# Block-sparse attention and SwiGLU on one core: scores issued a position earlier, gathers of V behind an exponential, and edge blocks sharing score matmuls

## The chip, the cores and the metric

The kernel runs on one core of a Trainium2 chip. The metric is the device time of one execution in microseconds (us).

## The reference

Two stages follow one another. First comes block-sparse attention over q, k and v of shape (4 batches, 8 heads, 768 positions, 64): the sequence is cut into 24 blocks of 32, and a query block sees its own block and the two beside it, the first and the last block, and three sampled blocks; the first and the last query block see everything.

```python
mask = np.abs(blk_i - blk_j) <= window
mask = mask | (blk_i == 0) | (blk_j == 0) | (blk_i == n_blocks - 1) | (blk_j == n_blocks - 1)
for qb in range(n_blocks):
    for kb in sampled_blocks[qb]:
        mask[qb * block:(qb + 1) * block, kb * block:(kb + 1) * block] = True
scores = np.where(mask, scores, -1000000000.0)
...
attn = attn / (np.sum(attn, axis=-1, keepdims=True) + 1e-09)
```

Its output, with the heads laid side by side, is x: 3072 tokens of 512. Then comes a feed-forward stage: RMS normalisation with a gain, two products with 512 x 1536 weights, SwiGLU, and a product with 1536 x 512 weights.

```python
rms = np.sqrt(np.mean(x * x, axis=-1, keepdims=True) + 1e-06)
xn = x / rms * rms_g
g = xn @ w_gate
silu = g * (1.0 / (1.0 + np.exp(-g)))
val = xn @ w_val
return (silu * val @ w_out).astype(np.float32)
```

## The kernel before

Everything is in bfloat16 with sums in float32. Batch 0 is computed densely with a mask, in three query groups, and fills the first 73 us or so; the change does not touch it. Batches 1 to 3 are cut into 18 chunks of four query blocks (128 rows). Fifteen chunks are narrow: four neighbouring blocks, whose 128 keys per block (window, first and last block, sampled blocks; each key row holds two neighbouring positions) are gathered into a tile of their own. Three are edge chunks, one in each batch: blocks 0, 23, 1 and 22, of which the first two see the whole sequence.

The order of the work is written out by hand. A loop runs over 19 steps (i = 0 to 18), each with ten positions (0 to 9). At each position it issues the jobs that were put down for it with `do(position, job)`, and then `position()` issues as many pieces of the feed-forward stage (FFN) as a rate says, so that TensorE has matrix work between the small pieces of attention. The FFN runs on groups of 2, 3, 4, 4, 3 and 2 chunks (256, 384 or 512 columns); its pieces are gate (gp, L737, then a tanh on ScalarE, th, L741), value (vp, L748, then two products on VectorE, u, L752, and hps, L756) and down (yp, L766, four pieces to a chunk, then ScalarE's yo, L771, and a store by SyncE's queue). Engines run their instructions in the order of issue.

What step i issues for chunk i, for the chunk before and for the one after (nx = i + 1):

- position 0: `values(i - 1)`, two halves of four heads (op, L644), on TensorE; positions 1 and 2: `normalise` of each half (rz, L669, and stage, L670) on VectorE; 4: `squares` (L677) on ScalarE; 5: `rms_power` (add L681, power L682) on GpSimd; 7: `x_scaled` (xs, L698 or L695) on VectorE, which reads the power, followed by a transposing DMA or, for some chunks, by transposes on TensorE.
- positions 1 to 4, in edge chunks 1 to 8: `scores(i, part)`. A part is one burst: eight score matmuls of 64 columns (L620) into one PSUM bank, and then at once the exponential of that bank on ScalarE (ex, L628), 512 columns. A narrow chunk has four parts of two heads, an edge chunk eight parts of one head. In an edge chunk's part, six of the eight matmuls go over the whole sequence (three thirds of the keys, straight from KT, for block 0 and for block 23) and two over gathered keys (kg) of blocks 1 and 22.
- for the next chunk: queries to a block-diagonal tile (`gather_q`, L500 or L503, VectorE, positions 3 and 5), window and edge keys (`gather_k`, L471 and L476, VectorE, positions 4 and 6), sampled keys (`sampled_k`, L485, GpSimd at position 0 and ScalarE spread over the step) and the rows of V (`gather_v`, L512): up to four indirect DMAs, issued by GpSimd at position 2. A tile of gathered V rows is used by every second chunk, so the gathers for chunk i + 1 wait for the values of chunk i - 1.
- for the next batch: loads on GpSimd's queue (L126, position 9), casts and transposes of keys and queries (L455 on TensorE, L457 on ScalarE), a table of V in DRAM.

Score, value, gate, down and transpose results share eight PSUM banks. `bank()` hands them out in a ring: three banks, one, and four more, in fixed order; whoever writes the bank next waits until its last reader is done. Three tiles hold exponentials (four parts each).

Of the kernel before, what the change touches and what calls it, by code (L numbers as in the profile page):

```python
# [18 lines left out]
def kernel(  # L19
# [495 lines left out]


# [89 lines left out]

    def bursts(i):
        return 8 if chunks[i][1][0] == 0 else 4

    def scores(i, part):  # L610
        b, qbs = chunks[i]
        wide = qbs[0] == 0
        heads = H // bursts(i)
        st = bank([P, 512], FP32, "st")
        at = 0
        for h in range(part * heads, (part + 1) * heads):
            of = [(KT[b % 2][:, h, cc::HC], j) for cc in range(HC) for j in range(2)] if wide else []
            of += [(kgs[i % 2][:, h, j, :], j) for j in range(2 if wide else 0, QB)]
            for lhsT, j in of:
                nc.tensor.matmul(  # L620
                    out=st[:, at:at + UN], lhsT=lhsT,
                    rhs=Qd[i % 2][:, h, :, :, j * HB:(j + 1) * HB].rearrange("p a w s -> p (a w) s"),
                    start=True, stop=True)
                at += UN
        if part % 4 == 0:
            exs[(i, part // 4)] = work.tile([P, 4 * 512], BF16, name="ex", tag="ex", bufs=3)
        ex = exs[(i, part // 4)][:, part % 4 * 512:(part % 4 + 1) * 512]
        nc.scalar.activation(  # L628
            out=ex.rearrange("p (u s w) -> p u s w", s=HB, w=2),
            in_=st.rearrange("p (u w s) -> p u s w", s=HB, w=2), func=AF.Exp, scale=SCALE)  # L630
# [3 lines left out]
    def values(i, g):  # L634
        b, qbs = chunks[i]
        wide = qbs[0] == 0
# [10 lines left out]
        for h in range(4 * g, 4 * g + 4):  # L647
            part = h // per
            ex = exs[(i, part // 4)][:, part % 4 * 512:(part % 4 + 1) * 512].rearrange(
                "p (h u w s) -> p h u w s", h=per, w=2, s=BLK)[:, h % per]  # L650
            if not wide:
# [3 lines left out]
                continue  # L655
            for n in range(NC):
                cc, w = divmod(n, 2)
                for j in range(2):
                    mm(h, j, ex[:, 2 * cc + j, w, :], Vs[b % 2][:, 2 * cc + w, h, :], n, NC)
                if n < 2:  # L660
                    for j in range(2, QB):
                        mm(h, j, ex[:, 4 + j, n, :], vg[:, j, n, h, :], n, 2)
# [415 lines left out]
    for i in range(NCH + 1):  # L1078
# [30 lines left out]
        if i < NCH:  # L1109
            n = bursts(i)  # L1110
            for part in range(n):
                do(1 + part, lambda part=part: scores(i, part))
# [10 lines left out]
        if nx is not None:  # L1123
# [20 lines left out]
            if nx > 1:  # L1144
                do(2, lambda: gather_v(nx))
# [51 lines left out]
```

## Time and profile before

| | us |
|---|---|
| median of three runs | 290.3 |
| lowest, highest | 289.85, 290.57 |
| the profiled execution, its own time | 290.28 |
| its span in the profile | 288.5 |

The span is the time from the first to the last instruction; 1.8 us of the profiled execution lie around it. The granted TensorE clock was 1.0 throughout. In the rows, PE is TensorE's matmuls, PEld its weight loads, DVE VectorE, ACT ScalarE, POOL GpSimd. A row of a timeline has the start, the duration, the engine, the line, the operation, its tiles (written <- read), the shape and a count; a bracket at its end has the idle time of the engine before it and what ended it. Tiles may show the name of a larger tile in which they lie: wide_q and wide_k hold the queries, keys and gathered keys of every second chunk. In a row of groups stand the total busy time and the mean of one in ns.

### The profile page before, as it was taken

The numbers are of one execution on the slowest core, as the hardware profiler recorded it, in microseconds if no ns is written. First come the engines' busy times: TensorE is split into PE (matmuls) and PEld (weight loads), VectorE is DVE, ScalarE is ACT, GpSimd is POOL, SyncE is SP. The second block draws the span as 40 slices with busy tenths as digits, with TensorE's granted clock in tenths as the row PEclk, the third lists the DMA queues.
The fourth block names the chain that finished last, engine by engine and source line by source line (L and its number), as shares of the span: only waits on it lengthen the run. The fifth ranks groups of instructions, "written<-read, shape, count | busy, mean of one in ns | idle before, by whom it ended". The sixth has DMA issues, their size and how long they took to land.

```text
span 288.5 us, 9875 instructions
## 1 busy us (share of the span) xinstructions
PE 273.9 (95%) x3840; PEld 185.3 (64%) x3871; DVE 216.7 (75%) x596; ACT 198.2 (69%) x467; POOL 146.7 (51%) x244
## 2 busy tenths in 40 slices
PE   8798999898999899799999999999999999999995
PEld 6586896687668678666665555545545556664783
DVE  7888889678979959966999578796499951784580
ACT  4896786588589789759989878577746484533331
POOL 8857244558487585787887627627723330101000
PEclk9999999999999999999999999999999999999999
DMA  7999999999885479898995845426932252000102
GB/s 133 287 214 201 206 207 268 290 229 315 168 232 125 142 205 287 173 222 259 250 170 154 280 122 154 101 73 186 204 115 77 59 168 77 36 2 36 75 1 73
DMA packets 37426, 47.44 MB, mean 164 GB/s; under 512 B 11184, under 2 KB 29380, under 8 KB 37380
## 3 DMA queue, kind: packets, MB, share of 16 engines
q0 software_dynamic: 21184, 32.60, 51.1%
q1 hardware_dynamic: 16132, 14.18, 17.2%
q8 instruction: 30, 0.49, 0.7%
q14 instruction: 16, 0.13, 0.1%
q10 hardware_dynamic: 64, 0.03, 0.0%
HBM read 46.45 MB, written 8.83 MB: 192 GB/s over the span
## 4 chain that ended last, share of the span: by engine, by line
PE 64%; DVE 16%; DMA 11%; issue 3%; POOL 3%; ACT 2%; DVEq 0%; ACTq 0%; POOLq 0%
PE yp L766 19%; PE gp L737 16%; PE vp L748 15%; PE st L620 5%; DMA gain<-in_moe_rms_g_dram 5%; DVE u L752 4%; DVE hps L756 4%; DMA qbf<-in_q_dram 4%; PE op L644 4%; DMA vraw<-in_v_dram 3%; PE tqk L455 2%; PE st L527 2%; DVE stage L670 1%; DVE xs L698 1%; PE op L536 1%
## 5 line engine op out<-in xcount | busy, mean ns | idle before, releaser
L512 POOL DMA_INDIRECT vg<-vtab,vidx x66 | 65.5, 992 | 45.2 <-PE op L644 27.1
L737 PE MATMUL gp<-xg,wg 128*128 128x256 bf16 (+2 forms) x426 | 80.2, 307 | 2.2 <-DVE stage L670 0.9
L748 PE MATMUL vp<-xg,wv 128*128 128x256 bf16 (+2 forms) x428 | 80.0, 307 | 1.4 <-DVE u L752 0.6
L741 ACT ACTIVATE th<-gp 128x256 bf16<-128x256 f32 (+2 forms) x108 | 49.8, 463 | 37.6 <-PE gp L737 34.4
L752 DVE SCALAR_TENSOR_TENSOR u<-th,gp 128x256 bf16<-128x256 bf16 (+2 forms) x108 | 54.5, 504 | 22.1 <-ACT th L741 21.5
L766 PE MATMUL yp<-wo,hps 128*128 128x512 bf16 (+1 forms) x282 | 69.1, 370 | 1.6 <-issue 0.3
L756 DVE TENSOR_TENSOR hps<-u,vp 128x256 bf16<-128x256 bf16 (+2 forms) x108 | 55.1, 510 | 11.6 <-PE vp L748 0.5
L628 ACT ACTIVATE ex<-st 128x512 bf16<-128x512 f32 x84 | 50.4, 600 | 13.8 <-PE st L620 12.6
L737 PEld LDWEIGHTS <-wg 128*128 128x128 bf16 x432 | 39.7, 98 | 20.0 <-issue 2.0
L748 PEld LDWEIGHTS <-wv 128*128 128x128 bf16 x432 | 39.5, 98 | 18.6 <-issue 1.5
L766 PEld LDWEIGHTS <-hps 128*128 128x128 bf16 x300 | 26.1, 98 | 20.8 <-DMA wo<-in_moe_w_out_dram 0.3
L530 ACT ACTIVATE ex<-st 128x768 bf16<-128x768 f32 x42 | 33.3, 813 | 5.8 <-PE st L527 5.6
L771 ACT ACTIVATE yo<-yp 128x512 f32<-128x512 f32 (+1 forms) x25 | 14.6, 582 | 19.7 <-PE yp L766 19.5
L681 POOL TENSOR_TENSOR ssq<-ssq,eps 128x1 f32<-128x1 f32 x18 | 4.3, 241 | 39.6 <-ACT junk L677 38.1
L527 PE MATMUL st<-wide_q,wide_k 88*128 88x256 bf16 x144 | 22.9, 272 | 1.5 <-DVE wide_q L345 1.1
L644 PEld LDWEIGHTS <-ex 128*32 128x32 bf16 x1344 | 13.6, 95 | 7.8 <-issue 7.8
L670 DVE TENSOR_TENSOR stage<-op,rz 128x256 bf16<-128x256 f32 x36 | 15.3, 425 | 1.2
L644 PE MATMUL op<-vg,ex 128*32 128x66 bf16 x1056 | 15.2, 195 | 1.0 <-DVE u L752 1.0
L527 PEld LDWEIGHTS <-wide_k 88*128 88x128 bf16 x144 | 13.0, 97 | 5.0 <-DVE wide_q L345 2.0
L620 PEld LDWEIGHTS <-kg 128*128 128x128 bf16 x272 | 12.7, 98 | 5.2 <-issue 0.3
L620 PEld LDWEIGHTS <-wide_q 128*128 128x128 bf16 x256 | 12.5, 98 | 5.3 <-issue 0.2
L620 PE MATMUL st<-wide_q 128*128 128x64 bf16 x256 | 15.1, 193 | 0.1
(147 smaller groups left out, 379.6 us busy)
## 6 DMA issues: line engine op xcount, KB each, us to landing
out_dram<-yo SPq DMA_DIRECT2D x20, 256.0 KB
vraw<-in_v_dram SPq DMA_DIRECT2D x12, 384.0 KB
kbf<-in_k_dram POOLq DMA_DIRECT2D x15, 192.0 KB, 5.7
vtab<-Vs POOLq DMA_DIRECT2D x3, 792.0 KB, 6.2
qbf<-in_q_dram POOLq DMA_DIRECT2D x12, 192.0 KB, 8.4
vraw<-in_v_dram POOLq DMA_DIRECT2D x4, 384.0 KB, 6.4
wg<-in_moe_w_gate_dram POOLq DMA_DIRECT2D x4, 384.0 KB, 10.6
wv<-in_moe_w_val_dram POOLq DMA_DIRECT2D x4, 384.0 KB
```

Of the source, the lines that this page charges most:

```text
L512: nc.gpsimd.indirect_dma_start(vgs[i % 2][:, j, :], None, vtab[b][:], bass.IndirectOffsetOnAxis(ap=vidx[:, qbs[j]:qbs[j] + 1], axis=0))
L527: nc.tensor.matmul(out=at[:, e], lhsT=KT0[0:KR, h, jt * P:(jt + 1) * P], rhs=QT0[0:KR, h, c0 * P:(c0 + 2) * P], start=True, stop=True)
L530: nc.scalar.activation(out=ex[:, 3 * part:3 * (part + 1), :], in_=at[:, 0:3], func=AF.Exp, scale=SCALE)
L620: nc.tensor.matmul(out=st[:, at:at + UN], lhsT=lhsT, rhs=Qd[i % 2][:, h, :, :, j * HB:(j + 1) * HB].rearrange("p a w s -> p (a w) s"), sta ...
L628: nc.scalar.activation(out=ex.rearrange("p (u s w) -> p u s w", s=HB, w=2), in_=st.rearrange("p (u w s) -> p u s w", s=HB, w=2), func=AF.E ...
L644: nc.tensor.matmul(out=op[j * BLK:(j + 1) * BLK, at:at + VW], lhsT=lhsT, rhs=rhs, start=(n == 0), stop=(n == of - 1))
L737: nc.tensor.matmul(out=gp[:, 0:tg], lhsT=wg[:, c, f * P:(f + 1) * P], rhs=xg[:, c, 0:tg], start=(c == 0), stop=(c == KD - 1))
L741: nc.scalar.activation(out=th[:, 0:tg], in_=gp[:, 0:tg], func=AF.Tanh, scale=0.5)
L748: nc.tensor.matmul(out=vp[:, 0:tg], lhsT=wv[:, c, f * P:(f + 1) * P], rhs=xg[:, c, 0:tg], start=(c == 0), stop=(c == KD - 1))
L752: nc.vector.scalar_tensor_tensor(out=u[:, 0:tg], in0=th[:, 0:tg], scalar=1.0, in1=gp[:, 0:tg], op0=ALU.add, op1=ALU.mult)
L756: nc.vector.tensor_tensor(out=hps[f][:, 0:tg], in0=u[:, 0:tg], in1=vp[:, 0:tg], op=ALU.mult)
L766: nc.tensor.matmul(out=yp, lhsT=hps[f][:, tt * P:(tt + 1) * P], rhs=wo[:, f, lo:hi], start=(f == 0), stop=(f == NF - 1))
```

## The change

Four things are done.

1. `scores` and the exponentials become two jobs. In narrow chunks the scores of parts 0 to 3 are issued at positions 0 to 3 (they stood at 1 to 4); in edge chunks at positions 0, 1, 1, 2, 3, 3, 4 and 5 (they stood at 1 to 8). The exponentials stay at 1 + part. In step 0 both stand one position later than that: scores at 1 to 4, exponentials at 2 to 5.
2. In an edge chunk a part's scores over the whole sequence are three matmuls of 128 columns, for blocks 0 and 23 together, in place of six of 64. The two over gathered keys keep 64 columns, which are now written as two runs of 32 side by side with those of the other block. The exponential reads and writes longer runs, and `values` reads the new layout.
3. From step 1 on, the gathers of V for the next chunk are preceded on GpSimd by a copy of one element of an exponential tile (`behind`): part 1 of this step, in edge chunks part 2. It is issued at position 3, in edge chunks 4, and so are the gathers for the next chunk's blocks 0 to 2; they stood at position 2.
4. The gather for the fourth block is issued at position 6, behind the add and the power of `rms_power` at position 5.

VectorE's order is the same in both programs; so is ScalarE's apart from step 0, and SyncE's. GpSimd has 16 instructions more, and 72 matmuls go with their weight loads.

```diff
--- before.py
+++ after.py
@@ -513,6 +513,11 @@
                     vgs[i % 2][:, j, :], None, vtab[b][:],
                     bass.IndirectOffsetOnAxis(ap=vidx[:, qbs[j]:qbs[j] + 1], axis=0))
 
+    gate = const.tile([1, 1], BF16, name="gate")
+
+    def behind(i, part):
+        nc.gpsimd.tensor_copy(out=gate, in_=exs[(i, part // 4)][0:1, part % 4 * 512:part % 4 * 512 + 1])
+
 
     def ex_tile():
         t = work.tile([P, 4 * 512], BF16, name="ex", tag="ex", bufs=3)
@@ -604,36 +609,53 @@
 
     exs = {}
 
+    banks = {}
+
+    def wide(i):
+        return chunks[i][1][0] == 0
+
     def bursts(i):
-        return 8 if chunks[i][1][0] == 0 else 4
+        return 8 if wide(i) else 4
 
     def scores(i, part):
+
         b, qbs = chunks[i]
-        wide = qbs[0] == 0
         heads = H // bursts(i)
-        st = bank([P, 512], FP32, "st")
-        at = 0
+        st = banks[(i, part)] = bank([P, 512], FP32, "st")
         for h in range(part * heads, (part + 1) * heads):
-            of = [(KT[b % 2][:, h, cc::HC], j) for cc in range(HC) for j in range(2)] if wide else []
-            of += [(kgs[i % 2][:, h, j, :], j) for j in range(2 if wide else 0, QB)]
-            for lhsT, j in of:
+            q = Qd[i % 2][:, h].rearrange("p a w s -> p (a w) s")
+            if wide(i):
+                for cc in range(HC):
+                    nc.tensor.matmul(
+                        out=st[:, 2 * cc * UN:2 * (cc + 1) * UN], lhsT=KT[b % 2][:, h, cc::HC],
+                        rhs=q[:, :, 0:2 * HB], start=True, stop=True)
+                for j in range(2, QB):
+                    nc.tensor.matmul(
+                        out=st[:, 2 * HC * UN:].rearrange("p (x j s) -> p x j s", j=2, s=HB)[
+                            :, :, j - 2, :],
+                        lhsT=kgs[i % 2][:, h, j, :], rhs=q[:, :, j * HB:(j + 1) * HB],
+                        start=True, stop=True)
+                continue
+            for j in range(QB):
+                at = ((h % heads) * QB + j) * UN
                 nc.tensor.matmul(
-                    out=st[:, at:at + UN], lhsT=lhsT,
-                    rhs=Qd[i % 2][:, h, :, :, j * HB:(j + 1) * HB].rearrange("p a w s -> p (a w) s"),
-                    start=True, stop=True)
-                at += UN
+                    out=st[:, at:at + UN], lhsT=kgs[i % 2][:, h, j, :],
+                    rhs=q[:, :, j * HB:(j + 1) * HB], start=True, stop=True)
+
+    def exponentials(i, part):
+        st = banks.pop((i, part))
         if part % 4 == 0:
             exs[(i, part // 4)] = work.tile([P, 4 * 512], BF16, name="ex", tag="ex", bufs=3)
         ex = exs[(i, part // 4)][:, part % 4 * 512:(part % 4 + 1) * 512]
+        n = 2 * HB if wide(i) else HB
         nc.scalar.activation(
-            out=ex.rearrange("p (u s w) -> p u s w", s=HB, w=2),
-            in_=st.rearrange("p (u w s) -> p u s w", s=HB, w=2), func=AF.Exp, scale=SCALE)
+            out=ex.rearrange("p (u s w) -> p u s w", s=n, w=2),
+            in_=st.rearrange("p (u w s) -> p u s w", s=n, w=2), func=AF.Exp, scale=SCALE)
 
     ops, stages, ssqs, rstds = {}, {}, {}, {}
 
     def values(i, g):
         b, qbs = chunks[i]
-        wide = qbs[0] == 0
         op = bank([P, 512], FP32, "op")
         ops.setdefault(i, []).append(op)
         vg = vgs[i % 2].rearrange("p j (w h x) -> p j w h x", w=2, h=H)
@@ -646,20 +668,21 @@
 
         for h in range(4 * g, 4 * g + 4):
             part = h // per
-            ex = exs[(i, part // 4)][:, part % 4 * 512:(part % 4 + 1) * 512].rearrange(
-                "p (h u w s) -> p h u w s", h=per, w=2, s=BLK)[:, h % per]
-            if not wide:
+            ex = exs[(i, part // 4)][:, part % 4 * 512:(part % 4 + 1) * 512]
+            if not wide(i):
+                ex = ex.rearrange("p (h j w s) -> p h j w s", h=per, j=QB, w=2)[:, h % per]
                 for w in range(2):
                     for j in range(QB):
                         mm(h, j, ex[:, j, w, :], vg[:, j, w, h, :], w, 2)
                 continue
+            ex = ex.rearrange("p (u w j s) -> p u w j s", w=2, j=2, s=BLK)
             for n in range(NC):
                 cc, w = divmod(n, 2)
                 for j in range(2):
-                    mm(h, j, ex[:, 2 * cc + j, w, :], Vs[b % 2][:, 2 * cc + w, h, :], n, NC)
+                    mm(h, j, ex[:, cc, w, j, :], Vs[b % 2][:, 2 * cc + w, h, :], n, NC)
                 if n < 2:
                     for j in range(2, QB):
-                        mm(h, j, ex[:, 4 + j, n, :], vg[:, j, n, h, :], n, 2)
+                        mm(h, j, ex[:, HC, n, j - 2, :], vg[:, j, n, h, :], n, 2)
 
     def normalise(i, g):
         if g == 0:
@@ -1107,9 +1130,12 @@
             if i - 2 in by_pe:
                 do(0, lambda: x_turned(i - 2))
         if i < NCH:
-            n = bursts(i)
-            for part in range(n):
-                do(1 + part, lambda part=part: scores(i, part))
+
+            at = [0, 1, 1, 2, 3, 3, 4, 5] if wide(i) else [0, 1, 2, 3]
+            for part, n in enumerate(at):
+                do(n + (i == 0), lambda part=part: scores(i, part))
+            for part in range(bursts(i)):
+                do(1 + part + (i == 0), lambda part=part: exponentials(i, part))
         if b + 1 < B and s <= NP:
             if s < NP:
                 do(9 if s == 0 else 0, lambda: cast_v(b + 1, s, act))
@@ -1142,7 +1168,10 @@
                 do(at + (m + 1) * (NPOS - 1 - at) // len(kact), x)
 
             if nx > 1:
-                do(2, lambda: gather_v(nx))
+                part = 2 if wide(i) else 1
+                do(2 + part, lambda: behind(i, part))
+                do(2 + part, lambda: gather_v(nx, (0, 1, 2)))
+                do(6, lambda: gather_v(nx, (3,)))
         for m in range(min(6, len(by_need)) if i < 2 else 0):
             do(m, next_address)
 
```

## The prediction

> **What bounds the kernel now.** I read the page's busy shares and its chain first, then busy time by stretches, then the waits, then timelines of those places where TensorE stands still. The profiled execution took 290.28 us, its span 288.5 (1.8 lie around it), and the median of the three runs shown is 290.3 (289.85 to 290.57). The sum below is made against 290.28, so it holds for the median as it stands.
>
> ```profile
> span 288.5 us, 9875 instructions
> ...
> PE 273.9 (95%) x3840; PEld 185.3 (64%) x3871; DVE 216.7 (75%) x596; ACT 198.2 (69%) x467; POOL 146.7 (51%) x244
> ...
> PE 64%; DVE 16%; DMA 11%; issue 3%; POOL 3%; ACT 2%; DVEq 0%; ACTq 0%; POOLq 0%
> ```
>
> TensorE is busy 95% of the span, and the chain that ended last is TensorE's for 64% and VectorE's for 16%; ScalarE has 2% of it and GpSimd 3%. What the change moves is mostly ScalarE's and GpSimd's waiting. So the first thing to see is that there is little to win: only time in which TensorE stands still, or VectorE's stretches of the chain.
>
> ```profile
> 82.00:97.00 15.00, 13.76 (x258) 11.87 (x244) 12.76 (x36) 14.17 (x41) 11.03 (x18) 1.00 0.66 182
> ...
> 107.00:126.00 19.00, 17.19 (x335) 13.93 (x334) 17.17 (x51) 16.72 (x48) 13.57 (x24) 1.00 0.91 241
> ...
> 134.00:157.00 23.00, 22.48 (x397) 14.77 (x396) 20.98 (x50) 21.21 (x57) 19.27 (x31) 1.00 0.87 181
> 157.00:254.00 97.00, 95.69 (x1360) 53.72 (x1380) 69.06 (x158) 64.17 (x160) 39.90 (x69) 1.00 0.45 127
> ```
>
> The columns after the length are PE, PEld, DVE, ACT and POOL; the 1.00 is the granted clock. In the first three stretches (57 us) VectorE is busy 85 to 91% and its timeline has no idle bracket: small FFN groups of 256 and 384 columns give it two operations on each pair of gate and value pieces, and the next chunk's copies come on top. These stretches end when VectorE ends. From 157 to 254 TensorE is busy 95.69 of 97 us and VectorE 71%: there only TensorE's own order counts.
>
> ```profile
> ACT ex L628 <- PE st L620: 12.6, 15, 2.7
> ...
> PE gp L737 <- ACT ex L628: 0.7, 1, 0.7
> ```
>
> Total, times, longest. Exponentials wait 12.6 us for scores, which the change takes away, but ScalarE is not the bound. The other way round, TensorE waits once, 0.69 us, for an exponential to free a bank.
>
> **The change part by part.** *Edge blocks share matmuls.* In each of 24 parts (3 edge chunks of 8), eight matmuls of 64 columns become three of 128 and two of 64, so 72 matmuls and 72 weight loads go.
>
> ```profile
> 118.06 0.34 PE L620 MATMUL st<-wide_q,KT 128*128 128x64 bf16 x6
> ```
> ```profile
> L620 PE MATMUL st<-wide_q,KT 128*128 128x64 bf16 x48 | 2.7, 193 | 0.0
> L620 PEld LDWEIGHTS <-KT 128*128 128x128 bf16 x96 | 5.1, 103 | 2.7 <-DVE stage L670 0.2
> ```
> ```profile
> 114.98 0.49 PE L455 MATMUL tqk<-ident,qbf 128*128 128x128 bf16 x6
> ```
> ```profile
> L455 PE MATMUL tqk<-ident,qbf 128*128 128x128 bf16 x72 | 6.0, 219 | 0.7 <-DVE u L752 0.6
> ```
>
> Six matmuls of 64 columns take 0.34 us and one of them 193 ns, so they start (0.34 − 0.193)/5 = 29 ns apart; for 128 columns (0.49 − 0.219)/5 = 54 ns. Loads of 103 ns each stand beside them without stretching this. Six by 29 become three by 54: 12 ns a part, 24 parts, −0.3 us. Bounds: if a load were exposed wherever it goes, −72 × 103 ns = −7.4; if the two remaining 64-column matmuls, which now write in strides, cost as much as 128 columns, 48 × 25 ns = +1.2 − 0.3. I take −0.3, since the 29 ns row is these very matmuls. The Trainium skill, "TensorE: Matmul & The Clock Gate", section "Back-to-back issue gap", says that in a stream of load and matmul pairs both set the spacing, about 81 ns for 128 columns; by it three pairs fewer in a part would be 0.24 us, 5.8 us in all (an estimate from that page). The rows here, 29 and 54 ns with a load for each matmul, do not agree. The exponential keeps its 512 elements; its longer runs change ScalarE, which these parts do not wait for.
>
> *Scores a position ahead.* Nothing is added, but each burst stands before an FFN piece instead of behind it, and its bank is held a position longer. So the bank that a burst or the next piece takes is a younger one, and TensorE waits for whoever frees it. I went through the order of banks step by step. **Step 2**:
>
> ```profile
> 94.64 0.60 PE L737 MATMUL gp<-xg,wg 128*128 128x256 bf16 x4 [0.69 <-ACT ex L628]
> 95.07 0.40 PE L620 MATMUL st<-Qd,kg 128*128 128x64 bf16 x8
> ```
> ```profile
> 94.47 0.42 DVE L670 TENSOR_TENSOR stage<-op,rz 128x256 bf16<-128x256 f32 x1
> ```
>
> The wait of 0.69 goes, but what is late next is this second normalising product: the fourth burst now takes its bank, free at 94.89. Burst (8 × 29 ns = 0.23) and gate piece (0.44 from 94.64 to 95.07) then end at 95.57; before, they ended at 95.31. So +0.26, not −0.69. **Step 5**, an edge chunk:
>
> ```profile
> 120.72 0.61 PE L737 MATMUL gp<-xg,wg 128*128 128x256 bf16 x4 [0.35 <-DVE stage L670]
> ...
> 121.52 0.60 PE L748 MATMUL vp<-xg,wv 128*128 128x256 bf16 x4
> ```
> ```profile
> 120.78 0.42 DVE L670 TENSOR_TENSOR stage<-op,rz 128x256 bf16<-128x256 f32 x1
> ```
>
> Before, a gate piece waits for the first product; now a later burst waits for the second, until 121.20, with one gate piece (0.44) still to come that before had run at 121.52: 121.20 + 0.44 − 121.52 = +0.12. **Steps 3 and 6**, where an FFN group ends and the next begins:
>
> ```profile
> 104.94 0.23 PE st L620 x8
> ```
> ```profile
> 105.01 0.60 ACT L771 ACTIVATE yo<-yp 128x512 f32<-128x512 f32 x1
> ...
> 106.78 0.40 ACT L741 ACTIVATE th<-gp 128x256 bf16<-128x256 f32 x1
> ```
> ```profile
> 107.21 0.42 DVE L752 SCALAR_TENSOR_TENSOR u<-th,gp 128x256 bf16<-128x256 bf16 x1 [3.20 <-ACT th L741]
> ```
> ```profile
> 134.40 0.56 DVE L752 SCALAR_TENSOR_TENSOR u<-th,gp 128x384 bf16<-128x384 bf16 x1 [2.11 <-ACT th L741]
> ```
>
> A VectorE stretch begins with the first u, which waits for a tanh, which on ScalarE stands behind the last yo, which waits for the last down piece. A burst of 0.23 us now stands before that piece instead of behind it: the stretch starts 0.23 later, twice, +0.46. **Step 9**:
>
> ```profile
> 155.01 0.81 PE L766 MATMUL yp<-wo,hps 128*128 128x512 bf16 x2 [0.16 <-DVE u L752]
> 155.67 0.39 PE L620 MATMUL st<-wide_q 128*128 128x64 bf16 x8
> 155.90 0.81 PE L766 MATMUL yp<-wo,hps 128*128 128x512 bf16 x3
> ```
> ```profile
> 155.06 0.56 DVE L756 TENSOR_TENSOR hps<-u,vp 128x384 bf16<-128x384 bf16 x1
> ```
>
> Now the down piece takes the bank that this product frees at 155.62 and runs 0.65 (the 155.01 piece's 155.67 − 155.01), to 156.27; before, the same work was done at 155.90: +0.37. **Steps 11 and 16** have a burst behind the second normalising product too:
>
> ```profile
> 175.93 0.42 DVE L670 TENSOR_TENSOR stage<-op,rz 128x256 bf16<-128x256 f32 x1
> ...
> 231.48 0.42 DVE L670 TENSOR_TENSOR stage<-op,rz 128x256 bf16<-128x256 f32 x1
> ```
>
> They end at 176.35 and 231.90. No row shows the wait; it lies between nothing and the product's 0.42 each, and since by the order TensorE arrives 0.1 to 0.2 ahead of these ends, I take +0.3 for both. That work is TensorE-bound, so it is not given back.
>
> *Gathers behind a gate, the RMS power ahead of the fourth.* GpSimd gets 16 copies of one element, which wait for the second exponential (third of an edge chunk) of this step; behind one of them stand three gathers, the power and the fourth gather, and VectorE's x_scaled (xs) waits for the power. Step 6 is the tightest:
>
> ```profile
> 130.53 0.60 ACT L628 ACTIVATE ex<-st 128x512 bf16<-128x512 f32 x1
> ```
> ```profile
> 127.00 1.06 POOL L512 DMA_INDIRECT vg<-vtab,vidx  x1 [0.17 <-issue]
> ...
> 130.90 0.97 POOL L512 DMA_INDIRECT vg<-vtab,vidx  x1 [0.30 <-issue]
> ```
> ```profile
> 136.11 0.77 DVE L698 SCALAR_TENSOR_TENSOR xs<-stage,rstd,gain 128x512 bf16<-128x512 bf16 x1
> ```
> ```profile
> L681 POOL TENSOR_TENSOR ssq<-ssq,eps 128x1 f32<-128x1 f32 x18 | 4.3, 241 | 39.6 <-ACT junk L677 38.1
> L682 POOL TENSOR_TENSOR rstd<-ssq,mhalf 128x1 f32<-128x1 f32 x18 | 11.1, 616 | 1.5 <-POOL ssq L681 0.2
> ```
>
> The exponential ends at 131.13. The gate copy has no row; priced by the nearest, the add of 128x1, it is 0.24 (between nothing and the power's 0.62, 16 times, 0 to 9.9 us of GpSimd, which is idle for half of the span). Three gathers take 130.90 − 127.00 = 3.9 with their gaps, add and power 0.86: the power is there at 136.13. VectorE comes to xs at 136.11, and 0.23 later by the transition above. So the gate costs nothing here, with 0.2 us to spare; uncovered, it would cost what it is late. The fourth gather, past the power, and the loads and key copies queued behind it have a whole step: its rows are read by the values of the step after next.
>
> *What moved gathers do to VectorE.*
>
> ```profile
> 113.27 0.92 DVE L503 COPY wide_q<-QN 64x256 bf16<-64x256 bf16 x4
> ...
> 115.36 1.38 DVE L503 COPY wide_q<-QN 64x256 bf16<-64x256 bf16 x4
> ```
>
> The same four copies of queries take 0.92 or 1.38 us, the second time beside GpSimd's work. Some six steps in the three stretches with two sets of copies each, every second one lengthened by some 0.3, make 1.8 us that could be won if gathers went elsewhere, or lost if more copies met them. Since as many gathers run as before in the same stretches, I take nothing. The Trainium skill, "SBUF — State Buffer", section "SBUF: two separate sides", has GpSimd and a VectorE operation in a two-port mode shut one another out for the whole instruction. That agrees in direction with the 0.46 us here; by it, where the gathers land among the copies would decide.
>
> **Sum**: −0.3 + 0.26 + 0.12 + 0.46 + 0.37 + 0.3 = +1.2, of which I round down to +1.1, since a delay ahead of a VectorE stretch can be partly taken up: 290.28 + 1.1 = 291.4 us.
>
> **The rivals.** (1) *Faster, about 288.9*: the gathers, three of them begun one or two positions later, come off VectorE's two-port copies, and the three stretches lose 1.8 us; sharing gives 0.3; the transitions keep +0.46 and steps 11 and 16 +0.3, while the bank waits of steps 2, 5 and 9, which end with VectorE work, move along with it: 290.28 − 1.8 − 0.3 + 0.46 + 0.3 = 288.9. For it: 0.92 against 1.38. Against: with a period of about 9 us and four gathers of 1.3 a step, they cover half of each step wherever they stand. It decides once more than about 1.2 us of lengthening goes. (2) *Nothing to be seen, about 290.4*: the change does not do what it says for time; VectorE's stretches swallow steps 2, 5 and half of 3 and 6, the rest against the sharing. (3) *Slower still, about 292.9*: the gate opens 1.0 to 1.4 us later than I put it, because the exponentials share ScalarE with yo, squares and key copies; the 0.2 us to spare in step 6, and as little in step 3, are gone, and VectorE waits at xs for 0.8 twice: 291.4 + 1.5. It decides from a power later than xs by the table of step 6. (4) *Weight loads are what TensorE pays for*: −7.4, 282.9. Against it, 29 ns beside a load of 103.
>
> **How the numbers follow.** A measurement of this kernel tells 0.3%, ±0.87 us, from no change: faster is under 289.43, slower over 291.17. Forecast 0.55 (290.7 to 292.4 by itself; 0.08 of it inside the 0.3%); rival 1 0.20; rival 2 0.10 (0.09 inside, 0.01 slower); rival 3 0.11; rival 4 0.04. Faster 0.20 + 0.04 = 0.24; same 0.08 + 0.09 = 0.17; slower 0.47 + 0.01 + 0.11 = 0.59. Leaving out rival 4, half of rival 1 below its point and the ends of rival 3, the range is 288.7 to 293.0; the dear strided writes (+1.2 on 291.4) lie in it.
>
> **What would show it.** Right: the 0.69 us wait for an exponential gone, and TensorE waiting for L670's line at the fourth burst of step 2 and in step 5; the first u of the two stretches 0.2 later; 64- and 128-column scores still 29 and 54 ns apart; no VectorE wait for the power before 157 us. Wrong: xs waiting for the power in steps 3 or 6 (rival 3), query copies shorter all through 82 to 157 us (rival 1), or TensorE's score time falling by more than 1 us (rival 4).

## The result and the profile after

The changed kernel takes 299.61 us (median of four runs, 297.88 to 301.37) against 290.08 (289.44 to 290.57): ratio 1.033, 95% interval 1.0266 to 1.0394. It is slower by 9.5 us where +1.1 was forecast, and lies outside the forecast range. Its profiled execution is the fastest of the four.

The page of the changed kernel, the lines that answer to those of before:

```profile
span 295.9 us, 9756 instructions
...
PE 276.6 (93%) x3770; PEld 186.7 (63%) x3799; DVE 216.6 (73%) x596; ACT 197.5 (67%) x467; POOL 150.5 (51%) x260
...
PE 63%; DVE 19%; POOL 5%; issue 5%; DMA 4%; ACT 3%; ACTq 1%; DVEq 0%; POOLq 0%
```

TensorE is busy 2.7 us longer and VectorE as long as before; the span is 7.4 us longer. So it is mostly waits that came, not work; VectorE and GpSimd have more of the chain (19 and 5% after 16 and 3%). The change is another program text, so its lines have other numbers: scores L629 to L641, exponentials L651, values L666, products L693, power L705, xs L718 and L721, transposing DMA L723, gate pieces L760, value pieces L771, u L775. The waits of the changed kernel (total, times, longest):

```profile
POOL gate L519 <- ACT ex L651: 42.8, 14, 7.8
...
DVE xs L721 <- POOL rstd L705: 8.7, 4, 4.8
...
DVE xs L718 <- POOL rstd L705: 2.5, 2, 1.8
...
PE op L666 <- DVE u L775: 1.4, 1, 1.4
PE gp L760 <- DMA xg<-xs: 1.2, 1, 1.2
PE st L629 <- DVE stage L693: 1.2, 3, 0.7
...
PE st L641 <- DVE u L775: 0.9, 2, 0.5
PE st L641 <- DVE stage L693: 0.8, 1, 0.8
PE vp L771 <- DVE stage L693: 0.7, 2, 0.4
```

and of before, for the same wait of xs:

```profile
DVE xs L698 <- POOL rstd L682: 2.5, 2, 2.4
...
DVE xs L695 <- POOL rstd L682: 0.5, 1, 0.5
```

Two things are to be seen. VectorE waits for the power 11.2 us (8.7 + 2.5) where it waited 3.0. And TensorE waits in many places, mostly 0.2 to 0.8 us each, for VectorE to free a bank, with one wait of 1.2 us for a transposed xs, which before does not have. Its granted clock is 1.0, so none of this is a slower TensorE.

### The profile page after: what moved, and what is told of

Same layout as the page of the kernel before. It is cut to its first block, busy times and chain, and to the rows that moved or that the text cites. A ratio compares the mean times of both kernels' runs of the same rounds, so it can differ in the third digit from the quotient of the medians.

```text
span 295.9 us, 9756 instructions
## 1 busy us (share of the span) xinstructions
PE 276.6 (93%) x3770; PEld 186.7 (63%) x3799; DVE 216.6 (73%) x596; ACT 197.5 (67%) x467; POOL 150.5 (51%) x260
## 4 chain that ended last, share of the span: by engine, by line
PE 63%; DVE 19%; POOL 5%; issue 5%; DMA 4%; ACT 3%; ACTq 1%; DVEq 0%; POOLq 0%
PE yp L789 18%; PE gp L760 15%; PE vp L771 15%; DVE hps L779 4%; DVE u L775 4%; PE st L641 4%; PE op L666 3%; DMA kbf<-in_k_dram 2%; PE st L532 2%; PE op L541 2%; PE tqk L455 2%; DVE xs L721 2%; DMA xg<-xs 1%; POOL vg L512 1%; DVE stage L693 1%
## 5 line engine op out<-in xcount | busy, mean ns | idle before, releaser
L771 PE MATMUL vp<-xg,wv 128*128 128x256 bf16 (+2 forms) x429 | 79.9, 307 | 2.4 <-DVE stage L693 0.7
L760 PE MATMUL gp<-xg,wg 128*128 128x256 bf16 (+2 forms) x426 | 79.9, 307 | 1.7 <-DMA xg<-xs 1.2
L512 POOL DMA_INDIRECT vg<-vtab,vidx x66 | 67.7, 1026 | 24.4 <-issue 8.2
L775 DVE SCALAR_TENSOR_TENSOR u<-th,gp 128x256 bf16<-128x256 bf16 (+2 forms) x108 | 54.5, 504 | 24.2 <-ACT th L764 23.6
L789 PE MATMUL yp<-wo,hps 128*128 128x512 bf16 (+1 forms) x283 | 68.2, 370 | 1.5 <-ACT ex L651 0.4
L651 ACT ACTIVATE ex<-st 128x512 bf16<-128x512 f32 x84 | 50.1, 600 | 8.9 <-PE st L641 7.0
L760 PEld LDWEIGHTS <-wg 128*128 128x128 bf16 x432 | 40.3, 98 | 21.0 <-DMA xg<-xs 1.7
L771 PEld LDWEIGHTS <-wv 128*128 128x128 bf16 x432 | 40.1, 98 | 20.8 <-issue 2.4
L789 PEld LDWEIGHTS <-hps 128*128 128x128 bf16 x300 | 26.7, 98 | 22.5 <-issue 0.9
L532 PE MATMUL st<-wide_q,wide_k 88*128 88x256 bf16 x144 | 23.5, 275 | 1.9 <-DVE wide_q L345 1.7
L519 POOL COPY gate<-ex 1x1 bf16<-1x1 bf16 x16 | 3.0, 189 | 42.8 <-ACT ex L651 42.8
L666 PEld LDWEIGHTS <-ex 128*32 128x32 bf16 x1344 | 13.5, 95 | 8.2 <-issue 8.2
L721 DVE SCALAR_TENSOR_TENSOR xs<-stage,rstd,gain 128x512 bf16<-128x512 bf16 x14 | 10.9, 779 | 8.7 <-POOL rstd L705 8.7
L666 PE MATMUL op<-vg,ex 128*32 128x66 bf16 x1056 | 15.3, 195 | 1.6 <-DVE u L775 1.4
L704 POOL TENSOR_TENSOR ssq<-ssq,eps 128x1 f32<-128x1 f32 x18 | 3.5, 197 | 25.6 <-ACT junk L700 25.2
L693 DVE TENSOR_TENSOR stage<-op,rz 128x256 bf16<-128x256 f32 x36 | 15.3, 424 | 1.2
L641 PEld LDWEIGHTS <-kg 128*128 128x128 bf16 x256 | 11.5, 98 | 5.7 <-DVE stage L693 1.1
```

The source lines that it names most:

```text
L512: nc.gpsimd.indirect_dma_start(vgs[i % 2][:, j, :], None, vtab[b][:], bass.IndirectOffsetOnAxis(ap=vidx[:, qbs[j]:qbs[j] + 1], axis=0))
L532: nc.tensor.matmul(out=at[:, e], lhsT=KT0[0:KR, h, jt * P:(jt + 1) * P], rhs=QT0[0:KR, h, c0 * P:(c0 + 2) * P], start=True, stop=True)
L641: nc.tensor.matmul(out=st[:, at:at + UN], lhsT=kgs[i % 2][:, h, j, :], rhs=q[:, :, j * HB:(j + 1) * HB], start=True, stop=True)
L651: nc.scalar.activation(out=ex.rearrange("p (u s w) -> p u s w", s=n, w=2), in_=st.rearrange("p (u w s) -> p u s w", s=n, w=2), func=AF.Exp ...
L666: nc.tensor.matmul(out=op[j * BLK:(j + 1) * BLK, at:at + VW], lhsT=lhsT, rhs=rhs, start=(n == 0), stop=(n == of - 1))
L760: nc.tensor.matmul(out=gp[:, 0:tg], lhsT=wg[:, c, f * P:(f + 1) * P], rhs=xg[:, c, 0:tg], start=(c == 0), stop=(c == KD - 1))
```

## The experiments

Theory **P**: the gate makes the RMS power late, and xs and all behind it with it. Rival **B**: scores issued a position earlier hold banks, and TensorE waits. After the first four runs came theory **F**: while the gathers' transfers are in flight, engines run short of instructions.

Runs fell on chips of two kinds for this kernel. Where the result was measured, and on two other occasions, before takes 290 us (the first kind); on three it takes 311 to 316 (the second). One chip was met twice, both times of the second kind (315.56 and 311.04); that the kind belongs to the chip rests on that. Each ratio, with its 95% interval, is to runs of before on the same chip and occasion.

| kernel | where before takes 290 | where before takes 311 to 316 |
|---|---|---|
| the change | 299.61, 1.033 (1.0266 to 1.0394) | 305.62, 0.9746 (0.9692 to 0.9801) |
| scores ahead and edge | 294.69, 1.0159 (1.0142 to 1.0177) | 1.0091; 1.0068; 1.0192 |
| gathers alone | not run | 0.9637; 0.9643; 0.9783 |
| edge alone | not run | 0.9924; 0.998 |
| no gate copy | 294.8, 1.0156 (1.0138 to 1.0174) | not run |
| gathers and edge | 297.84, 1.0232 (1.0187 to 1.0277) | not run |
| two gathers ahead of the power | 297.41, 1.0247 (1.0211 to 1.0284) | not run |
| step 13's gathers as before | 296.46, 1.0221 (1.0201 to 1.0242) | 299.94, 0.9692 (0.9652 to 0.9732) |
| all gathers behind the power | not run | 336.9, 1.0745 (1.0686 to 1.0803) |
| before without gathers | 288.59, 0.9949 (0.9931 to 0.9967) | not run |

### The scores' part: `ahead_and_edge`, `ahead_again`, `ahead_third`, `ahead_fourth`

The changed kernel with

```diff
-                part = 2 if wide(i) else 1
-                do(2 + part, lambda: behind(i, part))
-                do(2 + part, lambda: gather_v(nx, (0, 1, 2)))
-                do(6, lambda: gather_v(nx, (3,)))
+                do(2, lambda: gather_v(nx))
```

> The changed kernel with its V gathers as before (all at position 2, no gate, the power behind all of them): scores a position ahead and shared edge matmuls alone. Theory P: +1 to +4 us on before, by TensorE's waits for L693's products and for u alone, and no wait for the power that before does not have. Rival B: +6 us or more.

> Scores a position ahead and shared edge matmuls, the gathers as before, again. Both theories: on a chip with before at 290 us +1 to +4 us from TensorE's waits for banks; on one with 315 us the measured +3 again.

> Scores a position ahead and shared edge matmuls, gathers as before, for a chip on which before takes 290 us. Theory P: +1 to +4 us, all of it TensorE's waits for VectorE to free banks and no wait for a transposed xs. Rival B: +6 us or more. On a 315 us chip 317 again.

> Scores a position ahead and shared edge matmuls, gathers as before, again, for a chip on which before takes 290 us. Theory P: +1 to +4 us on before by waits for banks; less than the kernel without the gate copy (294.8), which issues its fourth gather later. Rival B: +6 us or more. On a chip of the other kind 316 again.

Measured: 317.62 (1.0054 to 1.0128), 316.86 (1.0029 to 1.0108) and 315.86 (1.0144 to 1.0241) on chips of the second kind, and 294.69 against 289.83 on one of the first: +4.9 us, a little over what P allowed and half of the loss. On the second kind it is 2 to 5 us. The trace of `ahead_fourth` gives the places. Its timeline in step 1, TensorE and VectorE:

```profile
82.62 0.31 PE L641 MATMUL st<-wide_q 128*128 128x64 bf16 x5 [0.31 <-ACT wide_q L485]
...
83.20 0.60 PE L760 MATMUL gp<-xg,wg 128*128 128x256 bf16 x4
```
```profile
88.15 0.42 DVE L775 SCALAR_TENSOR_TENSOR u<-th,gp 128x256 bf16<-128x256 bf16 x1 [0.42 <-ACT th L764]
```

The first burst stands ahead of the first pieces, and waits there for a key copy besides; gate pieces and tanh are later, and a VectorE stretch that had no idle bracket behind its first u gets one of 0.42. All that VectorE frees behind it is free later. In step 4 a burst that now comes a position earlier waits for ScalarE's copy of sampled keys, and in step 5 pieces wait for exponentials:

```profile
110.83 0.31 PE L641 MATMUL st<-Qd,kg 128*128 128x64 bf16 x5 [0.53 <-ACT kg L485]
...
124.82 0.60 PE L771 MATMUL vp<-xg,wv 128*128 128x256 bf16 x4 [0.24 <-ACT ex L651]
125.78 2.75 PE L789 MATMUL yp<-wo,hps 128*128 128x512 bf16 x11 [0.36 <-ACT ex L651]
```

### Shared edge matmuls: `edge_alone`, `edge_third`

The kernel of the last experiment, and scores with their exponentials at the old positions:

```diff
-            at = [0, 1, 1, 2, 3, 3, 4, 5] if wide(i) else [0, 1, 2, 3]
-            for part, n in enumerate(at):
-                do(n + (i == 0), lambda part=part: scores(i, part))
             for part in range(bursts(i)):
-                do(1 + part + (i == 0), lambda part=part: exponentials(i, part))
+                do(1 + part, lambda part=part: scores(i, part))
+                do(1 + part, lambda part=part: exponentials(i, part))
```

> The kernel before with shared edge matmuls alone; each burst's scores and exponential are issued together at the old positions, gathers as before. Theory P and rival B both: nothing that can be told from before, -0.6 to 0.3 us; 54 ns between starts of the 128-column score matmuls. If the 64-column matmuls that write two runs each are dear, or the new layout costs the values something: +0.9 or more.

> Shared edge matmuls alone, for a chip on which before takes 290 us: -0.8 to 0.2 us (the estimate was -0.3 by the starts 29 and 54 ns apart). On a 315 us chip 2.5 us under before again.

Measured: 313.03, 0.9924 (0.9876 to 0.9972), and 310.14, 0.998 (0.9938 to 1.0021). A part's five matmuls in the trace of `edge_alone`, and the piece behind them:

```profile
128.53 0.33 PE L629 MATMUL st<-wide_q,KT 128*128 128x128 bf16 x3
128.70 0.22 PE L633 MATMUL st<-wide_q 128*128 128x64 bf16 x2
128.75 0.60 PE L771 MATMUL vp<-xg,wv 128*128 128x256 bf16 x4
```

They take 0.22 us (128.53 to 128.75) against 8 × 29 ns = 0.23; 128-column matmuls start (0.33 − 0.219)/2 = 55 ns apart. The strided writes cost nothing that shows. As a time, 0.3 us is less than either run could tell: the first came out 2.5 us under before, where both theories allowed 0.6, and the second did not repeat it. It was not run on a chip of the first kind.

### The gathers' part: `gathers_alone`, `gathers_again`, `gathers_third`, `gathers_and_edge`

The kernel before with `gate`, `behind` and, in place of `do(2, lambda: gather_v(nx))`, the four lines that the first diff above takes away; `gathers_and_edge` is the changed kernel with the diff just shown.

> The kernel before with parts 3 and 4 of the change alone: gate copy, three gathers, power, fourth gather; scores and edge blocks as before. Theory P (the power is late, and VectorE waits for it at xs): most of the 9.5 us is here, so +4 to +7 us on before, with VectorE waiting for the power in steps 3 and 5 and TensorE waiting over 1 us for the transposed xs ahead of a gate piece after 200 us. Rival B (banks: the scores issued a position earlier make TensorE wait for VectorE to free their banks): at most +2 us here.

> The gathers' part of the change alone, again. Theory F: on a chip with before at 290 us there is little starvation to save, so it is slower than before by what the late power costs, +3 to +7 us; on one with 315 us it is some 12 us faster, as measured. Theory P: +4 to +7 us on any chip.

> The gathers' part of the change alone, for a chip on which before takes 290 us. Theory P (the gate makes the power late; from there VectorE's xs, the transposing DMA and the gate piece of the fifth FFN group in step 14): +6 to +9 us, TensorE waiting 1 to 4 us for the transposed xs in step 14. Rival B (the scores a position ahead cost most): +2 us or less. On a 315 us chip 302 again.

> The changed kernel with the scores issued where they were, together with their exponentials; gate, gathers and shared edge matmuls stay. Theory F with the bank waits of the scores' part: 3 us or more under the changed kernel, on a 315 us chip 299 to 302, which would beat before and the change; on a 290 us chip +3 to +6 us on before, by the power. If the scores a position ahead help where the gathers are gated: at or above the changed kernel.

Measured: 302.95 against 315.56 (0.9578 to 0.9697), 302.53 against 314.62 (0.9583 to 0.9703), 303.1 against 311.04 (0.9743 to 0.9822): on chips of the second kind this part gains 8 to 13 us, which P did not allow. On the first kind `gathers_and_edge` loses 7.6 us without any scores moved, more than F with the bank waits had it. Its TensorE row, the transposing DMA that the row waits for, and its stretches (length, then PE, PEld, DVE, ACT, POOL; the granted clock stands before the DMA share):

```profile
211.99 1.89 PE L760 MATMUL gp<-xg,wg 128*128 128x512 bf16 x4 [3.80 <-DMA xg<-xs]
```
```profile
205.16 2.37 SPq L723 DMA_TRANSPOSE xg<-xs  x1
```
```profile
206.00:212.00 6.00, 2.20 (x32) 1.34 (x30) 1.90 (x6) 3.73 (x11) 5.12 (x10) 0.86 1.00 171
212.00:217.10 5.10, 5.10 (x13) 1.80 (x14) 1.38 (x2) 0.78 (x2) 1.71 (x4) 0.50 0.57 210
```

Most of the loss is one place: in step 14 the first gate piece of the fifth FFN group waits 3.8 us for a transposed xs, and then TensorE runs at half its clock for 5.1 us, which costs some 2.5 more (an estimate: half of 5.1). Step 14, from its first value matmul to the next chunk's, is 6.5 us longer than in before, of 7.7 in the whole span. The mean busy share of the DMA engines from 206 to 212 us is 1.00. The six runs differ by the clock: two at a granted clock of 1.0 took 294.69 and 295.16, four at 0.987 to 0.993 took 297.39 to 298.69. So the parts do not simply add: 7.6 here and 4.9 for the scores make 12.5, against 9.5 for the change, and only with the two runs at full clock (+4.7) does the sum come near it.

### Without the gate copy, and with an earlier power: `no_gate`, `two_ahead`

```diff
-                do(2 + part, lambda: behind(i, part))
```
```diff
-                do(2 + part, lambda: gather_v(nx, (0, 1, 2)))
-                do(6, lambda: gather_v(nx, (3,)))
+                do(2 + part, lambda: gather_v(nx, (0, 1)))
+                do(6, lambda: gather_v(nx, (2, 3)))
```

> The changed kernel without the copy of one element: three gathers start as soon as the values of the chunk before the last let them, then the power, then the fourth. Theory F: on a 315 us chip the gain of the gathers goes, about 313 to 318 us (as with the old order of gathers, 317); on a 290 us chip the power comes early again and the time is that of the scores' part alone, +1 to +4 us on before. If the power ahead of the fourth gather were what gains on a 315 us chip, it stays at 305.

> The changed kernel with two gathers ahead of the power and two behind it, in place of three and one. Theory P: the power is 1.25 us earlier in each step, so VectorE's waits at xs (8.7 us in the first trace of the changed kernel) shrink by a half or more, and the time falls by 2 to 4 us. Theory F: the fourth gather's transfer moves 1.25 us towards the values of the next step; on a 315 us chip that takes back what the power gives, within 2 us of the changed kernel.

Measured on a chip of the first kind: 294.8 and 297.41. Without the copy the kernel is level with the scores' part alone (294.69), so the copy carries the whole of the gathers' cost, 4.8 us, and with it gone the power ahead of the fourth gather costs nothing that shows. The copy makes both the power and the gathers late; this run does not part the two. Its waits:

```profile
DVE xs L721 <- POOL rstd L705: 2.3, 2, 2.1
...
PE gp L760 <- DMA xg<-xs: 0.3, 1, 0.3
```

Two gathers ahead of the power, in place of three, give back 2.2 us, as P had it (the two intervals overlap, so this is not clear of noise). VectorE's waits for the power go from 11.2 to 6.4 us, less than the half that P asked for, and steps 3, 4, 5, 9 and 16 are 0.2 to 0.9 us shorter than in the change. But TensorE waits 2.27 us in step 14, more than the change's 1.24, and its clock drops too:

```profile
204.67 1.20 SPq L723 DMA_TRANSPOSE xg<-xs  x1
```
```profile
211.48 1.32 PE L760 MATMUL gp<-xg,wg 128*128 128x512 bf16 x4 [2.27 <-DMA xg<-xs]
212.59 1.91 PE L771 MATMUL vp<-xg,wv 128*128 128x512 bf16 x4
...
215.76 1.03 PE L771 MATMUL vp<-xg,wv 128*128 128x512 bf16 x4
```

Here it is not the lateness of xs alone: from the issue of the transfer to the piece are 6.81 us (204.67 to 211.48), and 6.83 in `gathers_and_edge` (205.16 to 211.99), where before needs 4.82 at most (below). Had the transfer taken no longer than in before, the two waits of 2.27 and 3.80 would be some 0.3 and 1.8 us (an estimate from these rows). What slows the transfer is not shown by a run of its own.

### One step's gathers as before: `old_at_13`, `old_at_13_again`

```diff
-                part = 2 if wide(i) else 1
...
+                if i == 13:
+                    do(2, lambda: gather_v(nx))
+                else:
+                    part = 2 if wide(i) else 1
...
```

> The changed kernel, with the gathers of step 13 alone issued as before (position 2, no gate, the power behind all four). Theory P: xs of chunk 12 is not late ahead of step 14, TensorE's wait for the transposed xs (1.2 us in the changed kernel's fastest run, 2.3 and 3.8 us with the clock at half behind it in two other kernels) goes, and the time falls from 299.6 to 295 to 297 us on a 290 us chip, with runs closer together. If that wait is hidden by something else, within 1 us of the changed kernel.

> The changed kernel with step 13's gathers as before, again, for a chip on which before takes 290 us. Theory P: 295 to 297 us against the changed kernel's 299.6, no wait of TensorE above 0.5 us for a transposed xs, and the clock at full speed in step 14. If not that wait, 299 or more. On a chip of the other kind (before at 311 to 315 us) 300 again.

Measured: 296.46 on the first kind (295.93 to 297.23), 3.1 us under the change and with runs closer together; the wait for a transposed xs is gone from its list. One step of sixteen carries a third of the change's loss. The edit takes away both the late power and the late gathers of that step. On the second kind 299.94, 0.9692 of before, against 0.9783 for the gathers alone on the same occasion.

### What the gathers do elsewhere: `before_same`, `after_same`, `power_first`, `no_gathers`

Before and the change unchanged; the change with `do(6, lambda: gather_v(nx))` in place of its four lines; and before with the gathers from chunk 4 on left out:

```diff
-            if nx > 1:
+            if nx == 2 or nx == 3:
```

> The kernel before, unchanged, for its trace on the chip of this comparison. Theory F (instruction supply: while the gathers' transfers are in flight, engines run out of instructions, and how much depends on the chip): where before takes about 315 us, its trace has 15 us or more of TensorE and weight-load idle time that no wait explains, most of it within 5 us after GpSimd's gathers; where it takes 290 us, as in the first trace, 12 to 16 us (all weight-load and matmul rows so marked). Theory P (the power alone) has nothing to say of it.

> The changed kernel, unchanged, beside before on one chip. Theory F: on a chip where before takes about 315 us it is level with before or faster (the gate keeps the gathers away from the values and first scores, which gathers alone turned into 12 us less there); on one where before takes 290 us it is some 9 us slower. Theory P: slower by some 9 us on both.

> The changed kernel with all its V gathers at position 6, behind the power, and no gate; scores a position ahead and shared edge matmuls stay. Theory P: the power is no longer behind any gather, so xs waits for it at most as in before, and the time is that of the scores' part alone, +1 to +4 us on before. Rival B: the same +6 us or more as with the gathers where they were. If gathers late in the step are themselves the trouble (rows that land too late for values), TensorE waits at values for their DMA and the time is above the changed kernel's.

> The kernel before without the gathers of V from chunk 4 on (54 or so of 66 are left out; the values read the rows gathered earlier). Theory F: on a chip where before takes about 315 us, TensorE's idle time that no wait explains goes with them, and the time comes near that of the first chip, 288 to 297 us; on one with 290 us, 286 to 290. Theory P has no reason for more than 3 us on either, since before's gathers stand on no chain.

Measured: 313.43 against 314.62, 305.62 (faster than before by 2.5%, interval 2.0 to 3.1), 336.9, and on a chip of the first kind 288.59. P had the change slower on both kinds, and the gathers behind the power 1 to 4 us over before; on the second kind it failed in both. Gathers all at the end of the step make 21 us over before there, and 19 over the scores' part alone; leaving them out gains only 1.6 on the first kind. TensorE's idle time that ends with no releaser ("issue"), before on the first kind:

```profile
PEld L644 <- issue: 7.8, 21, 1.1
...
PEld L737 <- issue: 2.0, 6, 0.8
...
PEld L748 <- issue: 1.5, 4, 0.7
```

before on the second (`before_same`, whose profiled run took 310.29 us at a granted clock of 1.0, so the clock is not what parts the two kinds):

```profile
PEld L644 <- issue: 10.7, 26, 1.2
...
PEld L748 <- issue: 7.8, 17, 1.6
...
PEld L737 <- issue: 5.1, 11, 2.1
PEld L620 <- issue: 4.7, 5, 1.5
...
PE gp L737 <- issue: 3.9, 5, 2.0
```

and all gathers behind the power (`power_first`; L666 is the values):

```profile
PEld L666 <- issue: 36.4, 68, 1.2
...
PE op L666 <- issue: 24.1, 42, 1.2
```

The idle time goes where the gathers go: 60.5 us of rows at the values when the gathers are issued just ahead of them (loads and matmuls overlap, so this is not 60 us of time). That a shortage of instructions is behind it is argued from rows that wait for nothing else, not shown; why the two kinds of chip differ stays open, and so does what leaving the gathers out would give on the second.

## Why the prediction was wrong

It forecast +1.2 for the scores and edges and nothing for the gathers. Measured on chips of the result's kind: +4.9, and +4.7 more with the gate and the moved gathers. Two steps of it failed: the sizes of the bank waits, and the gate at nothing.

**Edge matmuls, −0.3: right by the starts** of 29 and 55 ns, though no run can tell 0.3 us. Rival 4 (exposed loads) did not come; the 81 ns a matmul of the Trainium skill ("TensorE: Matmul & The Clock Gate", "Back-to-back issue gap") do not hold for these bursts.

**Bank waits of the scores: the mechanism was right, the sizes were not.** The wait of 0.69 us for an exponential went, and the fourth burst of step 2 waits for the second product, as forecast. But I had that product end at 94.89, its time in before, and it ended at 95.32. The changed kernel's rows:

```profile
95.39 0.41 PE L641 MATMUL st<-Qd,kg 128*128 128x64 bf16 x8 [0.79 <-DVE stage L693]
```
```profile
94.90 0.42 DVE L693 TENSOR_TENSOR stage<-op,rz 128x256 bf16<-128x256 f32 x1
```

From one chunk's first value matmul to the next, in the scores' part alone on the first kind against before: step 2 +0.74 (forecast 0.26), step 5 +1.04 (0.12), steps 11 and 16 +0.48 and +0.44 (0.3 for both), step 9 +0.10 (0.37). Steps 4, 7, 8, 12, 13 and 14, of which I said nothing, add 0.17 to 0.38 each, 1.52 in all; step 4's wait is shown above (a key copy), the others are not traced one by one. What failed here is two things: the time at which a bank comes free was taken from the old trace although the edit moves what frees it, and in step 5 I asked only for VectorE as the reader that frees a bank, not for the exponentials that now stay a position behind. A third was not asked at all: whether what an earlier burst reads, the key copies, is there. The transitions were right: the first u comes 0.21 and 0.34 later (forecast 0.23), though step 3 gives its part back (+0.01; step 6 is 0.16 longer).

**The gate at nothing: wrong.** The working was right for one step: in step 6 xs does not wait. Timeline of the changed kernel in step 6, and in step 3:

```profile
139.10 0.74 DVE L721 SCALAR_TENSOR_TENSOR xs<-stage,rstd,gain 128x512 bf16<-128x512 bf16 x1
```
```profile
104.92 0.18 POOL L519 COPY gate<-ex 1x1 bf16<-1x1 bf16 x1 [1.94 <-ACT ex L651]
105.64 0.98 POOL L512 DMA_INDIRECT vg<-vtab,vidx  x1 [0.54 <-issue]
...
109.42 0.56 POOL L705 TENSOR_TENSOR rstd<-ssq,mhalf 128x1 f32<-128x1 f32 x1
```
```profile
110.02 0.75 DVE L721 SCALAR_TENSOR_TENSOR xs<-stage,rstd,gain 128x512 bf16<-128x512 bf16 x1 [0.50 <-POOL rstd L705]
```

The gate copy takes 0.18 (I took 0.24), and gate to power 5.06 us (104.92 to 109.98), as my 5.0. But step 6 was not the tightest. The same sum in step 3 starts from the second exponential of before, which ended at 104.05: 104.05 + 5.0 = 109.05, against xs at 108.07, late by 0.7 even with the transition's 0.23. I made the sum once and named "as little in step 3" without making it.

Worse, I looked only at VectorE's stretches. Past 157 us VectorE idles ahead of xs, so a late xs seemed free. It is not VectorE that waits there but what xs starts. The changed kernel, step 13 and 14:

```profile
207.69 0.75 DVE L721 SCALAR_TENSOR_TENSOR xs<-stage,rstd,gain 128x512 bf16<-128x512 bf16 x1 [4.76 <-POOL rstd L705]
```
```profile
208.47 1.96 SPq L723 DMA_TRANSPOSE xg<-xs  x1
```
```profile
212.84 1.04 PE L760 MATMUL gp<-xg,wg 128*128 128x512 bf16 x4 [1.24 <-DMA xg<-xs]
```

and before, at the same place:

```profile
201.85 1.20 SPq L700 DMA_TRANSPOSE xg<-xs  x1
```
```profile
206.67 1.03 PE L737 MATMUL gp<-xg,wg 128*128 128x512 bf16 x4
```

Before had 206.67 − 201.85 = 4.8 us from that transfer's issue to the piece that needs it, without a wait; after, the issue comes so late, and itself takes 1.96 in place of 1.20, that TensorE waits. With step 13's gathers as before, 3.1 of the 9.5 us are gone by the medians, and step 14 is as long as in the scores' part alone (in the change's profiled run, its fastest, it is 1.48 longer). The rest of the gate's 4.7 lies mainly in steps 3, 5, 9 and 16, which are 0.27 to 0.71 longer than in the scores' part alone, 1.9 together, of which steps 6, 7 and 8 give 0.8 back.

**Moved gathers and VectorE's copies at nothing: the row did not show what I read.** When the four copies took 1.38 us, GpSimd was issuing a load and copying keys; no gather was being issued. Rival 1's 1.8 us had no other row.

**The rivals.** Rival 3, at 0.11 and with +1.5 as its price, has the sign that came, a power later than xs, but not the reason: in step 3 the gate opened 3.96 us after the step's first value matmul (104.92 less 100.96), where before has 3.86 for the end of that exponential (104.05 less 100.19), so ScalarE did not make it late. Its point of decision was met in step 3 by before's own rows, and the wait of TensorE in step 14 is not in it. Rival 1's gain did not come: VectorE is busy 216.6 us after 216.7. The range ended at 293.0, since I priced the unknown ends of the scores' part by one product's 0.42 us in two steps, and not in every step.

## What to carry to other kernels

When an edit moves the producer of a wait, the time at which it ends moves as well: follow a delay through the engines (burst, gate piece, tanh, VectorE, bank) before a place is priced, and make the sum for every step of the loop, not for the one that looks tightest. A late result on an engine with idle time is free only if the next one that reads it, over a DMA too, has time: count from the issue of that DMA to its first reader, and allow for a longer transfer (6.8 us here, where before needed 4.8 at most). Run the parts on more than one chip where DMA traffic is in play: here the same edit lost 3% on one kind and won 2.5% on another.

## What the runs showed of the hardware

A stall of TensorE of 3.80 us (`gathers_and_edge`) was followed by 5.1 us at half the granted clock, one of 2.27 us (`two_ahead`) by pieces of 1.91 in place of 1.03 us, one of 1.24 us (the change) by none. Stretches of the first two, cut where the clock changes:

```profile
208.19:210.29 2.10, 0.00 (x1) 0.00 (x0) 0.00 (x0) 1.73 (x5) 1.60 (x2) 1.00 0.79 117
210.29:211.99 1.70, 0.00 (x0) 0.00 (x1) 0.00 (x0) 0.00 (x0) 1.49 (x3) 0.50 0.87 305
```
```profile
211.48:212.10 0.62, 0.62 (x3) 0.30 (x4) 0.00 (x0) 0.00 (x0) 0.45 (x2) 1.00 1.04 393
212.10:215.51 3.41, 3.41 (x9) 1.22 (x8) 1.37 (x2) 0.78 (x2) 2.18 (x4) 0.50 0.82 261
```

The Trainium skill, "TensorE: Matmul & The Clock Gate", section "What's actually happening", has the clock fall after an idle window of about 3.4 us. Neither trace agrees, since no 3.4 us of idle time stand ahead of the fall: the clock fell 2.10 us into the first stall, and 0.62 us after the end of the second, which was 2.27 long. It stayed at half for 6.83 us (to 217.12) and for 3.41.

The same program took 290 us on chips of one kind and 311 to 316 on the other; in the two lists of waits of before, the rows of TensorE's matmuls and weight loads that end with no releaser add up to 14.9 and 42.7 us. The transposing DMA took 1.20 us to issue in before's step 13, and 1.96 in the changed kernel's; over its 14 issues it is 1.19 to 2.33 in the one and 1.19 to 2.34 in the other, and what lengthens it stays open.
